# A decode kernel for gated attention and feed-forward: the sum of the exponentials moved from the end of a group to the next group's join with V

## The chip, the cores and the metric

The kernel runs on one core of a Trainium2 chip. The metric is the device time of one execution in microseconds (us); smaller is better. Engines: TensorE (PE) multiplies matrices, VectorE (DVE) and ScalarE (ACT) work element by element, GpSimd (POOL) only sets constants and merges two semaphores here, and SyncE (SP) issues every transfer from HBM. The engines run side by side and meet only at semaphores.

## The reference

One token passes through an attention block with cached keys and values (32 query heads, 8 key/value groups, 32,768 positions of width 128) and through a gated feed-forward block; a scalar gate mixes both.

```python
g = sigmoid((x * gate_w).sum(-1))
q = x @ wq                                # 32 heads of 128
scores = einsum(q, k) * 128 ** -0.5       # per group: 4 heads, 32768 keys
p = softmax(scores)
a = einsum(p, v) @ wo
b = (silu(x @ w_gate) * (x @ w_up)) @ w_down
return g * a + (1 - g) * b
```

K and V are 8 groups of 8.39 MB each, all in bf16, and are read once.

## The kernel before

SBUF holds five pages of 4.19 MB. Two of them hold a group's K in turn (pages A and B for odd groups, B and C for even ones) and two hold V. One loop over the eight groups runs on each engine (`Fori` in steps of `STEP` = 16, so that one semaphore can count all groups).

In each group TensorE first does `emit_k`. A *fill* is eight fp32 transposes of K from a page into one of two PSUM tiles `pst` (L334); VectorE copies each to SBUF (`ktT`, L695); TensorE then multiplies it with the queries into the scores `ps_sc` (L346), two fills behind (`LAG`). There are 16 fills in a group, eight (`UPP`) from each page; page B is read first. After K comes `emit_v` for the group *before*: 64 matmuls of the exponentials `ET` with V into `ps_o` (L401), which this text calls the join. ACT copies the join to `acc` (L576), and `emit_reduce` (L424) folds it to `ps_m`. `emit_max` (L381, L385) turns the row maxima into one maximum per head on all partitions; VectorE makes the bias `nbias` from it (L721), and ACT computes the 32,768 exponentials of the four heads in eight instructions (L583), each with its sum in `esum`.

Last in the group is `emit_sum`. VectorE adds the two halves of `esum` to `esum2` (L733), TensorE sums it over the partitions (L413, into the bank of the scores), VectorE takes the reciprocal (L737) and multiplies it with the gate (L739). Since TensorE runs in program order, the fills of the next K stand behind this sum, and so behind all exponentials of the group.

SyncE issues transfers in the order K(0), K(1), V(0), K(2), V(1), K(3), V(2) and so on, with a wait before each:

```python
if g > 1:
    sp.wait_ge(sem_fill, UPG * (g - 1) + UPP + (g == 2))   # load_k, L277
...
if g:
    sp.wait_ge(sem_v_free, STEP * (g + 1))                 # load_v
```

K(g) goes when page B of the group before has been read, that is 8 fills into group g-1; for K(2) one fill later, 25 in all instead of 24. V(g) goes when the join of V(g-1) is done. The last V goes in two halves, page by page, then the down weights `wd`, and behind the seventh join the output weights `wo` in five pieces (L326).

After the loop `emit_end` joins the last V, folds it, multiplies by `wd`; VectorE scales by the reciprocals (L749), transposes, and TensorE runs through the pieces of `wo` as they land (L223, L234). One copy (L770) and one transfer end the kernel.

Of the kernel before, what the change touches and what calls it, by code (L numbers as in the profile page):

```python
# [5 lines left out]
ACT = mybir.ActivationFunctionType  # L6
# [6 lines left out]
def bass_gated_mix__gqa_block_cached__swiglu_ffn__decode_kernel(  # L13
# [37 lines left out]
    LAG = 2  # L51
# [26 lines left out]
    with ExitStack() as es:  # L78
        def S_(name):
            return es.enter_context(nc.semaphore(name))  # L80
# [39 lines left out]
        sem_nbias = S_("s_nbias")  # L120
        sem_exp = S_("s_exp")
        sem_v_free = S_("s_v_free")
        sem_es = S_("s_es")
        sem_s = S_("s_s")
        sem_acc = S_("s_acc")
        sem_red = S_("s_red")
        sem_rc = S_("s_rc")
        sem_dve_oT1 = S_("s_dve_oT1")
        sem_dve_oT2 = S_("s_dve_oT2")
# [36 lines left out]
        nbias = T("nbias", [128, HPG], FP32)  # L166
        esum = T("esum", [128, NB, HPG], FP32)
        eone = T("eone", [128, 1], FP32)
        esum2 = T("esum2", [128, HPG], FP32)
        acc = T("acc", [128, RQ, DH], FP32)  # L170
        rS = T("rS", [128, HPG], FP32)
        rSw = T("rSw", [128, (G + 1) * STEP], FP32)
        oTw = T("oTw", [128, (G + 2) * STEP], FP32)
        oTs = T("oTs", [128, H], BF16)
        O2a = T("O2a", [128, WOJ], BF16)
        O2 = T("O2", [128, WOJ], BF16)
# [10 lines left out]
        M_A0 = 0  # L187
        M_B0 = M_A0 + 128
        M_P0 = M_B0 + HPG
        M_T0 = M_P0 + HPG  # L190
        M_O0 = M_T0 + FC
        M_X0 = M_O0 + WOJ
        M_G0 = M_X0 + KC
# [1 line left out]

        ps_i = ps_sc[0][:, 0:128]
        ps_c = ps_sc[0][:, :]
        ps_s = ps_sc[1][:, 0:HPG]
        ps_d = ps_sc[1][:, 0:128]

        strip_sel = ident[:, :].rearrange("p (s x) -> p s x", s=NSTRIP)[:, :, 0]
# [55 lines left out]
        with nc.Block("main") as block:  # L257
# [13 lines left out]
            def _(sp):  # L271
                def load_k(g):
                    lo = PG_A if g % 2 else PG_B
                    dst = page[:, lo : lo + NB, :].rearrange("p b (r d) -> p b r d", d=DH)
                    src = A_k_cache[0, g, :, :].rearrange("(p b r) d -> p b r d", b=NB, r=R)
                    if g > 1:
                        sp.wait_ge(sem_fill, UPG * (g - 1) + UPP + (g == 2))  # L277
                        sp.dma_start(
                            dst.rearrange("p b r d -> p (b r d)"),
                            src.rearrange("p b r d -> p (b r d)"),  # L280
                        ).then_inc(sem_k[0], 16)
                        return
                    for b in range(NB):
                        first = lo + b == PG_B
                        if g and first:
                            sp.wait_ge(sem_fill, UPP)
                        sp.dma_start(dst[:, b, :, :], src[:, b, :, :]).then_inc(
                            sem_k[0] if first else sem_k1 if g else sem_k[1], 16
                        )
# [39 lines left out]
            def _(pe):  # L329
# [25 lines left out]
                def emit_k(i):  # L355
                    pe.wait_ge(sem_k[0], i + 16)
                    for n in range(UPP):
                        if n >= LAG:
                            pe.wait_ge(sem_cp, i + (n - LAG + 1))
                        emit_fill(PG_B, n)  # L360
                        if n >= LAG:
                            emit_scores(0, n - LAG)
                    pe.wait_ge(sem_k[1], i + 16)
                    odd = i & STEP
                    for n in range(UPP, UPG + LAG, LAG):
                        if n < UPG:
                            for pg in (PG_A, PG_C):
                                with pe.If(odd > 0) if pg == PG_A else pe.Else():
                                    for m in range(n, n + LAG):
                                        pe.wait_ge(sem_cp, i + (m - LAG + 1))  # L370
                                        emit_fill(pg, m - UPP)
                        else:
                            pe.wait_ge(sem_cp, i + UPG)
                        for m in range(n - LAG, n):
                            ins = emit_scores(m // UPP, m % UPP)
                            if m % UPP == UPP - 1:
                                ins.then_inc(sem_sc, UPP)
# [30 lines left out]
                            )  # L408
                    ins.then_inc(sem_v_free, STEP)

                def emit_sum(i):
                    pe.wait_ge(sem_es, i + STEP)
                    pe.matmul(  # L413
                        ps_s,
                        ones_f[:, :],
                        esum2[:, :],
                        start=True,
                        stop=True,
                    ).then_inc(sem_s, STEP)

                def emit_reduce(n):
                    pe.wait_ge(sem_acc, n)
                    for q in range(RQ):
                        ins = pe.matmul(  # L424
                            ps_m[:, M_P0 : M_P0 + HPG],
                            acc[:, q, :],
                            sel4[:, q * HPG : (q + 1) * HPG],
                            start=(q == 0),
                            stop=(q == RQ - 1),
                        )  # L430
                    ins.then_inc(sem_red, STEP)

                def emit_start():
# [84 lines left out]
                    pe.wait_ge(sem_ps0, 1)  # L518
                    pe.wait_ge(sem_dve_tT, 1)
                    for n, sem in enumerate((sem_v_free, sem_red)):  # L520
                        c = M_P0 + 2 * n
                        pe.matmul(
                            ps_m[:, c : c + 2],
                            ones_f[0:1, :],
                            ones_f[0:1, 0:2],
                            start=True,
                            stop=True,
                        ).then_inc(sem, STEP)

                    with pe.Fori(0, G * STEP, STEP) as i:  # L530
                        emit_k(i)
                        with pe.If(i > 0):
                            emit_v(
                                [[(sem_v, i), (sem_exp, i)], []], (PG_V, PG_V + 1)
                            )
                            emit_reduce(i + STEP)
                        emit_max(i)
                        emit_sum(i)

                def emit_end():  # L540
                    emit_v(
                        [[(sem_exp, G * STEP), (sem_vl[0], 16)], [(sem_vl[1], 16)]], PG_L
                    )
                    emit_reduce((G + 1) * STEP)
                    pe.wait_ge(sem_ld_wd, 16)
                    for j in range(FC):
# [16 lines left out]
            def _(act):  # L563
# [5 lines left out]
                act.activation(sg, pst[1][:, 0:FS], ACT.Sigmoid).then_inc(sem_act_sg, 1)  # L569

                act.wait_ge(sem_ones, 2)
                act.activation(eone[:, :], ones_f[:, 0:1], ACT.Exp)

                with act.Fori(0, G * STEP, STEP) as i:
                    act.wait_ge(sem_v_free, i + STEP)
# [19 lines left out]
            def _(dve):  # L595
# [92 lines left out]
                dve.wait_ge(sem_pe_t, 1)  # L688
                dve.tensor_copy(tT[:, :], ps_m[:, M_T0 : M_T0 + FC]).then_inc(sem_dve_tT, 1)

                with dve.Fori(0, G * STEP, STEP) as i:
                    for n in range(UPG + 1):
                        if n < UPG:
# [18 lines left out]
                    dve.wait_ge(sem_t, i + STEP)  # L712
                    dve.tensor_reduce(  # L713
                        gm[:, :], ps_m[0:HPG, M_A0 : M_A0 + 128], AX.X, ALU.max
                    ).then_inc(sem_d, 1)
                    dve.wait_ge(sem_d, i + 3)
                    dve.tensor_scalar(  # L717
                        diag[:, :], ident_f[0:HPG, 0:HPG], gm[:, 0:1], None, op0=ALU.mult
                    ).then_inc(sem_dg, STEP)
# [1 line left out]
                    dve.tensor_scalar(  # L721
                        nbias[:, :], ps_m[:, M_B0 : M_B0 + HPG], -SCALE, None, op0=ALU.mult
                    ).then_inc(sem_nbias, STEP)
                    dve.wait_ge(sem_red, i + STEP)
                    dve.tensor_scalar(
                        oTw[:, bass.ds(i, HPG)],
                        ps_m[:, M_P0 : M_P0 + HPG],
                        1.0,
                        None,
                        op0=ALU.mult,  # L730
                    ).then_inc(sem_rc, STEP)
                    dve.wait_ge(sem_exp, i + STEP)
                    dve.tensor_tensor(  # L733
                        esum2[:, :], esum[:, 0, :], esum[:, 1, :], ALU.add
                    ).then_inc(sem_es, STEP)
                    dve.wait_ge(sem_s, i + STEP)
                    dve.reciprocal(rS[:, :], ps_s).then_inc(sem_d, 1)  # L737
                    dve.wait_ge(sem_d, i + 4)
                    dve.tensor_scalar(  # L739
                        rSw[:, bass.ds(i, HPG)], rS[:, :], g_col[:, 0:1], None, op0=ALU.mult  # L740
                    ).then_inc(sem_d, STEP - 4)

                dve.wait_ge(sem_red, (G + 1) * STEP)
                dve.tensor_copy(
                    oTw[:, G * STEP : G * STEP + HPG], ps_m[:, M_P0 : M_P0 + HPG]
                ).then_inc(sem_rc, STEP)
                dve.wait_ge(sem_rc, (G + 1) * STEP)
                dve.wait_ge(sem_d, G * STEP)
                dve.tensor_tensor(  # L749
                    oTs[:, :].rearrange("p (g h) -> p g h", h=HPG),  # L750
                    oTw[:, STEP : (G + 1) * STEP].rearrange("p (g x) -> p g x", x=STEP)[:, :, 0:HPG],
                    rSw[:, 0 : G * STEP].rearrange("p (g x) -> p g x", x=STEP)[:, :, 0:HPG],
                    ALU.mult,
                ).then_inc(sem_dve_oT1, 1)
                dve.wait_ge(sem_dve_oT1, 1)
                dve.transpose(O2a[:, :], oTs[:, :]).then_inc(sem_dve_oT2, 1)
# [48 lines left out]
```

## Time and profile before

| | |
|---|---|
| median of three runs | 353.12 us (352.42 to 355.97) |
| profiled execution: time / span | 353.74 us / 352.4 us |
| busy, share of the span: PE, PEld, DVE, ACT | 75%, 63%, 54%, 9% |
| mean granted TensorE clock | 0.831 |
| moved by the DMA queue | 148.12 MB, 97.9% of 16 engines' span |

The span runs from the first to the last instruction on the core. PE is a matmul, PEld the load of its stationary operand, which overlaps it. A row of a group or of the timeline gives line, engine, operation, result and operands, count and time; in square brackets or behind the last bar stands the idle time just before and what ended it. A plain fp32 matmul shows as two passes ("x2").

### The profile page before, as it was taken

Reading aid. Unit: us, or ns where it says so; the run is one execution under the profiler, and the core shown is the slowest. Engines: PE = TensorE matmul, PEld = TensorE weight load, DVE = VectorE, ACT = ScalarE, POOL = GpSimd, SP = SyncE. Lnnn points to the kernel's source line nnn. Section 1 sums busy time; section 2 is a strip of 40 time slices with the busy share of each in tenths; the row PEclk is TensorE's granted clock in tenths of the full one; section 3 lists DMA queues with packets and bytes.
Section 4 is the critical chain, followed back from the end, with each engine's and each line's share of the span. In section 5 each row is a group of like instructions: output and inputs, shape, how many; then the busy total and the mean of one; then the engine's idle time right before and its main releaser. Section 6 shows DMA issues by size and latency. Waiting matters only on the chain.

```text
span 352.4 us, 8780 instructions
## 1 busy us (share of the span) xinstructions
PE 263.5 (75%) x3875; PEld 221.1 (63%) x3875; DVE 190.0 (54%) x251; ACT 33.4 (9%) x143; POOL 0.4 (0%) x6
## 2 busy tenths in 40 slices
PE   1445994399939995899759983999379963999383
PEld 1125994399529972898359942996279843995231
DVE  4134894199417960598129921795149921894100
ACT  1002000300040002100030003000400012000400
POOL 0000000000000000000000000000000000000000
PEclk9975898589887996699759985898859995898878
DMA  8999999998899999998998998999999989989996
GB/s 340 400 448 420 456 424 438 433 402 335 379 476 439 394 476 402 431 476 372 461 469 365 476 461 372 476 439 394 476 402 431 476 365 469 469 365 435 419 422 241
DMA packets 4051, 148.22 MB, mean 421 GB/s; under 512 B 458, under 2 KB 460, under 8 KB 844
## 3 DMA queue, kind: packets, MB, share of 16 engines
q1 hardware_dynamic: 4044, 148.12, 97.9%
q8 instruction: 6, 0.10, 0.1%
q14 instruction: 1, 0.01, 0.0%
HBM read 148.11 MB, written 0.00 MB: 420 GB/s over the span
## 4 chain that ended last, share of the span: by engine, by line
DMA 45%; PE 44%; issue 4%; DVE 3%; ACT 2%; SPq 1%; ACTq 0%; DVEq 0%
DMA page<-in_A_k_cache_dram 39%; PE pst L334 30%; PE ps_sc L346 8%; DMA page<-in_A_wo_dram 6%; PE ps_o L401 4%; ACT ET L583 2%; DVE ktT L695 2%; PE ps_m L424 1%; PE ps_sc L413 0%; SPq L326 0%; PE ps_m L385 0%; ACT acc L576 0%; DVE gm L713 0%; SPq L311 0%; ACTq L583 0%
## 5 line engine op out<-in xcount | busy, mean ns | idle before, releaser
L695 DVE COPY ktT<-pst 128x2048 bf16<-128x2048 bf16 x128 | 153.5, 1221 | 34.8 <-PE pst L334 30.5
L334 PE MATMUL pst<-ident_f,page 128*128 128x128 f32 x1024 | 148.8, 301 | 7.6 <-DMA page<-in_A_k_cache_dram 6.4
L334 PEld LDWEIGHTS pst<-ident_f,page 128*128 128x128 f32 x1024 | 127.7, 156 | 11.5 <-DMA page<-in_A_k_cache_dram 6.9
L346 PE MATMUL ps_sc<-qcur,ktT 128*128 128x8 bf16 x2048 | 64.2, 166 | 6.3 <-DVE ktT L695 6.3
L346 PEld LDWEIGHTS ps_sc<-qcur,ktT 128*128 128x128 bf16 x2048 | 63.8, 97 | 8.0 <-DVE ktT L695 7.0
L401 PE MATMUL ps_o<-page,ET 128*16 128x512 bf16 x512 | 41.2, 494 | 0.4 <-issue 0.4
L401 PEld LDWEIGHTS ps_o<-page,ET 128*16 128x16 bf16 x512 | 15.1, 110 | 22.7 <-issue 16.5
L583 ACT ACTIVATE ET<-ps_sc,nbias 128x128 bf16 x64 | 23.9, 556 | 52.3 <-DVE nbias L721 52.3
L413 PE MATMUL ps_sc<-esum,ones_f 128*128 128x4 f32 x16 | 4.5, 351 | 31.1 <-DVE esum L733 31.1
L576 ACT ACTIVATE acc<-ps_o 128x512 f32<-128x512 f32 x8 | 4.8, 597 | 223.9 <-PE ps_o L401 219.9
L713 DVE TENSOR_REDUCE gm<-ps_m 4x1 f32<-4x128 f32 x8 | 2.2, 278 | 43.9 <-PE ps_m L381 43.9
L413 PEld LDWEIGHTS ps_sc<-esum,ones_f 128*128 128x128 f32 x16 | 4.0, 312 | 31.5 <-issue 31.5
L583 ACT ACTIVATION_READ_ACCUMULATOR ET<-ps_sc,nbias 128x1 f32 x64 | 18.3, 286 | 0.0
L703 DVE TENSOR_REDUCE pmaxf<-ps_sc 128x4 f32<-128x512 f32 x16 | 11.0, 686 | 8.4 <-PE ps_sc L346 8.4
L733 DVE TENSOR_TENSOR esum<-esum 128x4 f32<-128x4 f32 x8 | 1.3, 162 | 25.4 <-ACT ET L583 25.4
L424 PEld LDWEIGHTS ps_m<-sel,acc 128*128 128x128 f32 x64 | 7.7, 191 | 10.1 <-ACT acc L576 8.9
L424 PE MATMUL ps_m<-sel,acc 128*128 128x4 f32 x64 | 8.4, 255 | 6.1 <-ACT acc L576 5.3
L385 PE MATMUL ps_m<-diag,ones_f 4*128 4x4 f32 x16 | 3.6, 294 | 6.3 <-DVE diag L717 6.3
L385 PEld LDWEIGHTS ps_m<-diag,ones_f 4*128 4x128 f32 x16 | 3.2, 244 | 7.8 <-issue 7.8
L445 PE MATMUL ps_m<-ones_bf,x_row 1*128 1x1 bf16 x4 | 0.3, 172 | 9.3 <-DMA x_row<-in_A_x_dram 9.3
L445 PEld LDWEIGHTS ps_m<-ones_bf,x_row 1*128 1x128 bf16 x4 | 0.2, 115 | 9.6 <-DMA x_row<-in_A_x_dram 9.6
L381 PE MATMUL ps_m<-ident_f,pmax 128*4 128x128 f32 x8 | 2.3, 282 | 3.7 <-issue 3.7
(73 smaller groups left out, 53.6 us busy)
## 6 DMA issues: line engine op xcount, KB each, us to landing
page<-in_A_k_cache_dram SPq DMA_DIRECT2D x4, 4096.0 KB, 34.5
page<-in_A_v_cache_dram SPq DMA_DIRECT2D x2, 4096.0 KB, 27.9
page<-in_A_wq_dram SPq DMA_DIRECT2D x1, 4096.0 KB, 13.4
page<-in_A_wo_dram SPq DMA_DIRECT2D x1, 2048.0 KB, 18.3
page<-in_B_w_gate_dram SPq DMA_DIRECT2D x1, 1792.0 KB, 16.6
page<-in_B_w_up_dram SPq DMA_DIRECT2D x1, 1792.0 KB, 20.5
wd<-in_B_w_down_dram SPq DMA_DIRECT2D x1, 1792.0 KB, 20.8
page<-in_A_wo_dram SPq DMA_DIRECT2D x1, 1024.0 KB, 20.4
```

The source lines that it names most:

```text
L334: ins = pe.transpose(pst[u % NST][:, k * 128 : (k + 1) * 128], kv[:, n * 128 : (n + 1) * 128], ident_f[:, :],)
L346: ins = pe.matmul(ps_sc[b][:, col : col + 2 * HPG], kt[:, k, e, :], qcur[:, e, :], start=(e == 0), stop=(e == 1),)
L381: pe.transpose(ps_m[0:HPG, M_A0 : M_A0 + 128], pmax[:, :], ident_f[:, :]).then_inc(sem_t, STEP)
L385: pe.matmul(ps_m[:, M_B0 : M_B0 + HPG], ones_f[0:HPG, :], diag[:, :], start=True, stop=True,).then_inc(sem_b, STEP)
L401: ins = pe.matmul(ps_o[32 * c : 32 * c + RQ * HPG, :], ET[:, n : n + RQ, :].rearrange("p n h -> p (n h)"), v[:, k * RQ : (k + 1) * RQ, :], ...
L413: pe.matmul(ps_s, ones_f[:, :], esum2[:, :], start=True, stop=True,).then_inc(sem_s, STEP)
L424: ins = pe.matmul(ps_m[:, M_P0 : M_P0 + HPG], acc[:, q, :], sel4[:, q * HPG : (q + 1) * HPG], start=(q == 0), stop=(q == RQ - 1),)
L576: act.activation(part, ps_o[:, :], ACT.Copy).then_inc(sem_acc, STEP)
L583: act.activation(ET[:, b * R : (b + 1) * R, h], sc[:, h, bass.ds(bank, R)], ACT.Exp, bias=nbias[:, h : h + 1], scale=SCALE, accum_out=esum ...
L695: dve.tensor_copy(ktT[:, n % NKT, :], pst[n % NST][:, :].bitcast(BF16)).then_inc(sem_cp, 1)
L703: dve.tensor_reduce(pmaxf[:, b, :], sc, AX.X, ALU.max).then_inc(sem_d, 1)
L713: dve.tensor_reduce(gm[:, :], ps_m[0:HPG, M_A0 : M_A0 + 128], AX.X, ALU.max).then_inc(sem_d, 1)
```

## The change

- `emit_sum`, `esum2`, `ps_s` and their semaphores go. TensorE goes from the maximum of a group at once to the next group's fills.
- The sum over the partitions is now two accumulating matmuls in `emit_reduce`, one for each half of `esum`, into a column range of its own in `ps_m`. They run one group later, beside the join of the same group's V, ahead of the wait for `acc`.
- Since the next group's scores overwrite what the exponentials read, TensorE waits for `sem_exp` ahead of the first scores of a group, behind its third fill. ACT's first exponential (`eone`) gives the initial count.
- VectorE makes the result of a group in two operations, `emit_out`: the reciprocal from `ps_m`, then one `scalar_tensor_tensor` (fold times gate times reciprocal). It stands after `nbias`, and once after the loop. The scaling of all groups at the end becomes a copy.
- K(2) is issued after 24 fills.

```diff
-                        sp.wait_ge(sem_fill, UPG * (g - 1) + UPP + (g == 2))
+                        sp.wait_ge(sem_fill, UPG * (g - 1) + UPP)
...
                         emit_fill(PG_B, n)
+                        if n == LAG:
+                            pe.wait_ge(sem_exp, i + STEP)
                         if n >= LAG:
                             emit_scores(0, n - LAG)
...
-                def emit_sum(i):
-                    pe.wait_ge(sem_es, i + STEP)
-                    pe.matmul(ps_s, ones_f[:, :], esum2[:, :], ...).then_inc(sem_s, STEP)
                 def emit_reduce(n):
+                    for b in range(NB):
+                        pe.matmul(
+                            ps_m[:, M_S0 : M_S0 + HPG],
+                            ones_f[:, :],
+                            esum[:, b, :],
+                            start=(b == 0),
+                            stop=(b == NB - 1),
+                        )
                     pe.wait_ge(sem_acc, n)
...
                             emit_reduce(i + STEP)
                         emit_max(i)
-                        emit_sum(i)
...
-                        [[(sem_exp, G * STEP), (sem_vl[0], 16)], [(sem_vl[1], 16)]], PG_L
+                        [[(sem_exp, (G + 1) * STEP), (sem_vl[0], 16)], [(sem_vl[1], 16)]], PG_L
+                    pe.wait_ge(sem_rc, G * STEP)
                     emit_reduce((G + 1) * STEP)
...
-                act.activation(eone[:, :], ones_f[:, 0:1], ACT.Exp)
+                act.activation(eone[:, :], ones_f[:, 0:1], ACT.Exp).then_inc(sem_exp, STEP)
...
+                def emit_out(i, at):
+                    dve.wait_ge(sem_red, i + STEP)
+                    dve.reciprocal(rS[:, :], ps_m[:, M_S0 : M_S0 + HPG]).then_inc(sem_rs, STEP)
+                    dve.wait_ge(sem_rs, i + STEP)
+                    dve.scalar_tensor_tensor(
+                        oTw[:, at], ps_m[:, M_P0 : M_P0 + HPG], g_col[:, 0:1], rS[:, :],
+                        ALU.mult, ALU.mult,
+                    ).then_inc(sem_rc, STEP)
...
-                    (wait sem_red, scale oTw; wait sem_exp, esum2 = esum[0] + esum[1];
-                     wait sem_s, rS = 1 / ps_s; rSw = rS * g_col)
+                    emit_out(i, bass.ds(i, HPG))
+                emit_out(G * STEP, slice(G * STEP, G * STEP + HPG))
...
-                dve.tensor_tensor(oTs, oTw, rSw, ALU.mult)
+                dve.tensor_copy(oTs, oTw)
```

(The lines in round brackets and the last two are shortened.)

More of the change, by code (lines that the diff above doesn't have):

```diff
@@ L122, in bass_gated_mix__gqa_block_cached__swiglu_ffn__decode_kernel @@
         sem_v_free = S_("s_v_free")
-        sem_es = S_("s_es")
-        sem_s = S_("s_s")
         sem_acc = S_("s_acc")
         sem_red = S_("s_red")
+        sem_rs = S_("s_rs")
         sem_rc = S_("s_rc")
@@ L168, in bass_gated_mix__gqa_block_cached__swiglu_ffn__decode_kernel @@
         eone = T("eone", [128, 1], FP32)
-        esum2 = T("esum2", [128, HPG], FP32)
         acc = T("acc", [128, RQ, DH], FP32)
         rS = T("rS", [128, HPG], FP32)
-        rSw = T("rSw", [128, (G + 1) * STEP], FP32)
-        oTw = T("oTw", [128, (G + 2) * STEP], FP32)
+        oTw = T("oTw", [128, (G + 2) * STEP], BF16)
         oTs = T("oTs", [128, H], BF16)
@@ L189, in bass_gated_mix__gqa_block_cached__swiglu_ffn__decode_kernel @@
         M_P0 = M_B0 + HPG
-        M_T0 = M_P0 + HPG
+        M_S0 = M_P0 + HPG
+        M_T0 = M_S0 + HPG
         M_O0 = M_T0 + FC
@@ L197, in bass_gated_mix__gqa_block_cached__swiglu_ffn__decode_kernel @@
         ps_c = ps_sc[0][:, :]
-        ps_s = ps_sc[1][:, 0:HPG]
         ps_d = ps_sc[1][:, 0:128]
@@ L409, in emit_v @@
                     ins.then_inc(sem_v_free, STEP)
-                def emit_sum(i):
-                    pe.wait_ge(sem_es, i + STEP)
[L413 to L419, printed above, removed]
-                def emit_reduce(n):
+                def emit_reduce(n):
+                    for b in range(NB):
[6 more added lines that the diff above has]
+                        )
                     pe.wait_ge(sem_acc, n)
@@ L520, in emit_start @@
                     for n, sem in enumerate((sem_v_free, sem_red)):
-                        c = M_P0 + 2 * n
+                        c = M_P0 + HPG * n
                         pe.matmul(
-                            ps_m[:, c : c + 2],
+                            ps_m[:, c : c + HPG],
                             ones_f[0:1, :],
-                            ones_f[0:1, 0:2],
+                            ones_f[0:1, 0:HPG],
                             start=True,
@@ L533, in emit_start @@
                             emit_v(
-                                [[(sem_v, i), (sem_exp, i)], []], (PG_V, PG_V + 1)
+                                [[(sem_v, i)], []], (PG_V, PG_V + 1)
                             )
@@ L689, in _ @@
                 dve.tensor_copy(tT[:, :], ps_m[:, M_T0 : M_T0 + FC]).then_inc(sem_dve_tT, 1)
+                def emit_out(i, at):
[3 more added lines that the diff above has]
+                    dve.scalar_tensor_tensor(
+                        oTw[:, at],
+                        ps_m[:, M_P0 : M_P0 + HPG],
+                        g_col[:, 0:1],
+                        rS[:, :],
+                        ALU.mult,
+                        ALU.mult,
+                    ).then_inc(sem_rc, STEP)
                 with dve.Fori(0, G * STEP, STEP) as i:
@@ L714, in _ @@
                         gm[:, :], ps_m[0:HPG, M_A0 : M_A0 + 128], AX.X, ALU.max
-                    ).then_inc(sem_d, 1)
-                    dve.wait_ge(sem_d, i + 3)
+                    ).then_inc(sem_d, STEP - 2)
+                    dve.wait_ge(sem_d, i + STEP)
                     dve.tensor_scalar(
@@ L723, in _ @@
                     ).then_inc(sem_nbias, STEP)
[L724 to L749, printed above, removed]
+                    emit_out(i, bass.ds(i, HPG))
+                emit_out(G * STEP, slice(G * STEP, G * STEP + HPG))
+                dve.wait_ge(sem_rc, (G + 1) * STEP)
+                dve.tensor_copy(
                     oTs[:, :].rearrange("p (g h) -> p g h", h=HPG),
-                    oTw[:, STEP : (G + 1) * STEP].rearrange("p (g x) -> p g x", x=STEP)[:, :, 0:HPG],
-                    rSw[:, 0 : G * STEP].rearrange("p (g x) -> p g x", x=STEP)[:, :, 0:HPG],
-                    ALU.mult,
+                    oTw[:, STEP : (G + 1) * STEP].rearrange("p (g x) -> p g x", x=STEP)[
+                        :, :, 0:HPG
+                    ],
                 ).then_inc(sem_dve_oT1, 1)
```

## The prediction

> **What bounds the kernel now.** I read the page's totals first, then its DMA parts, because no engine is busy for more than 75% of the span.
>
> ```profile
> span 352.4 us, 8780 instructions
> PE 263.5 (75%) x3875; PEld 221.1 (63%) x3875; DVE 190.0 (54%) x251; ACT 33.4 (9%) x143; POOL 0.4 (0%) x6
> ...
> q1 hardware_dynamic: 4044, 148.12, 97.9%
> ```
>
> One queue moves 148.12 MB and its packets fill 97.9% of the span of all 16 DMA engines. That points to a transfer-bound kernel, so the next view is the table of windows: does the stream ever stop? Columns: the window in us, its length, busy time of each engine, TensorE clock, DMA share, GB/s (a packet counts where it starts).
>
> ```profile
> 40.00:78.00 38.00, 27.91 (x441) 26.64 (x440) 24.69 (x30) 3.00 (x16) 0.00 (x0) 0.82 1.02 435
> 78.00:79.00 1.00, 1.00 (x23) 0.99 (x22) 0.91 (x2) 0.00 (x0) 0.00 (x0) 1.00 0.91 393
> 79.00:80.00 1.00, 1.00 (x22) 0.99 (x21) 0.91 (x2) 0.00 (x0) 0.00 (x0) 1.00 0.00 0
> 80.00:81.00 1.00, 1.00 (x17) 0.90 (x13) 1.00 (x1) 0.00 (x0) 0.00 (x0) 1.00 0.00 0
> 81.00:82.00 1.00, 0.99 (x10) 0.86 (x9) 0.91 (x2) 0.00 (x0) 0.00 (x0) 1.00 0.00 0
> 82.00:140.00 58.00, 47.87 (x747) 39.70 (x745) 32.94 (x43) 5.26 (x25) 0.00 (x0) 0.86 1.01 434
> 140.00:200.00 60.00, 51.12 (x741) 46.32 (x742) 38.60 (x44) 5.51 (x29) 0.00 (x0) 0.82 1.01 437
> 200.00:260.00 60.00, 44.21 (x660) 35.94 (x657) 28.07 (x41) 7.18 (x34) 0.00 (x0) 0.80 1.01 436
> ```
>
> The stream runs at 434 to 437 GB/s and stops exactly once, from 79 to 82 us. The issues of the SyncE queue and the time from issue to landing say why. First the timeline of the queue, then, in the same order, the landing rows of those five issues (last number: us to landing).
>
> ```profile
> 44.67 0.33 SPq L287 DMA_DIRECT2D page<-in_A_k_cache_dram  x1
> 45.04 0.43 SPq L298 DMA_DIRECT2D page<-in_A_v_cache_dram  x1
> 81.17 0.33 SPq L278 DMA_DIRECT2D page<-in_A_k_cache_dram  x1
> 97.94 0.33 SPq L298 DMA_DIRECT2D page<-in_A_v_cache_dram  x1
> 117.11 0.33 SPq L278 DMA_DIRECT2D page<-in_A_k_cache_dram  x1
> ```
>
> ```profile
> page<-in_A_k_cache_dram SPq DMA_DIRECT2D x1, 4096.0 KB, 17.3
> page<-in_A_v_cache_dram SPq DMA_DIRECT2D x1, 36.3
> page<-in_A_k_cache_dram SPq DMA_DIRECT2D x1, 22.1
> page<-in_A_v_cache_dram SPq DMA_DIRECT2D x1, 24.6
> page<-in_A_k_cache_dram SPq DMA_DIRECT2D x1, 24.8
> ```
>
> Issue plus landing time gives the landings: second half of K(1) 61.97, V(0) 81.34, K(2) 103.27, V(1) 122.54, K(3) 141.91. The steps between them are 19.37, **21.93**, 19.27 and 19.37 us. V and K of a group are 8.39 MB each, so 19.34 us is the streaming time of one and K(2) cost 2.59 us more: it was issued at 81.17, when V(0) was already at its end. Its lone landing time of 22.1 is 19.34 plus 2.76 of start and completion that nothing covered. So a transfer loses nothing if it is issued 2.76 us before its predecessor lands; for K(2) that is by 78.58.
>
> **The change, part by part.** The waits of the engines show what the removed sum cost TensorE, and what it already waits for beside it.
>
> ```profile
> PE ps_sc L413 <- DVE esum L733: 31.1, 8, 3.9
> PE pst L334 <- DMA page<-in_A_k_cache_dram: 6.4, 4, 2.8
> ```
>
> 31.1 us of TensorE idle time in eight groups look like a large prize. But the second row says that in four of the groups TensorE, once past the sum, waits for K all the same, and the stream between 82 and 260 us never pauses. A TensorE that is ready earlier then only waits longer for K. The one place where its lateness stops the stream is K(2), which waits for fills of group 1. The timeline of TensorE and the exponentials (ACT) there:
>
> ```profile
> 63.46 0.56 PE L385 MATMUL ps_m<-diag,ones_f 4*128 4x4 f32 x2 [0.79 <-DVE diag L717]
> 64.49 0.55 ACT L583 ACTIVATE ET<-ps_sc,nbias 128x128 bf16 x1 [31.76 <-DVE nbias L721]
> 67.17 0.31 ACT L583 ACTIVATION_READ_ACCUMULATOR ET<-ps_sc,nbias 128x1 f32 x1
> 67.90 0.56 PE L413 MATMUL ps_sc<-esum,ones_f 128*128 128x4 f32 x2 [3.88 <-DVE esum L733]
> 68.39 4.88 PE L334 MATMUL pst<-ident_f,page 128*128 128x128 f32 x24
> 78.75 1.07 PE L334 MATMUL pst<-ident_f,page 128*128 128x128 f32 x8
> 80.07 2.17 PE L334 MATMUL pst<-ident_f,page 128*128 128x128 f32 x16
> ```
>
> *Next K at once.* Fills of group 1 start 0.49 us after the start of the sum's two passes (67.90 to 68.39). With the sum gone, the same two-pass broadcast of the maximum at 63.46 is last, and K(1) has been there since 61.97: fills start at 63.95, **4.44 us sooner**. The new wait, for all exponentials before the first scores, stands behind three fills: these end at 63.95 + 4.88 = 68.83, the exponentials at 67.48, so it costs nothing with 1.35 us to spare. Were that cover gone it would delay the fourth fill, and with it K(2), by the excess. The copies of the first fills now run while ACT reads its scores, which the trace of before does not show; bound: nothing, up to a doubling of the 2.99 us of exponentials, which would hold the scores 1.64 us. I take nothing, and the slack below covers the other end.
>
> *K(2) after 24 fills.* A fill is eight passes: 16 fills belong to group 0, three to the 24 passes from 68.39, then one every 1.31 us, so the row at 78.75 is fill 24, ending at 79.82, and the first half of the row at 80.07 is fill 25, behind which K(2) went at 81.17. One fill fewer is 1.35 us sooner. With both edits K(2) is issued at 81.17 - 1.35 - 4.44 = **75.38**, 3.2 us ahead of 78.58. "At once" alone gives 76.73, also early enough; 24 fills alone give 79.82 and leave 1.24 us of the gap. So the second edit adds nothing beyond the first; together they remove the whole 2.59.
>
> *The sum moved beside V's join.* Two fp32 products per group (two passes each) go in ahead of the wait for ACT's copy of the join. The rows that price them and their cover, with the end of the kernel, where alone they lie near the last chain:
>
> ```profile
> 334.40 5.81 PE L401 MATMUL ps_o<-page,ET 128*16 128x512 bf16 x64 [0.39 <-issue]
> 340.97 1.05 PE L424 MATMUL ps_m<-sel,acc 128*128 128x4 f32 x8 [0.76 <-ACT acc L592]
> 342.13 0.16 DVE L744 COPY oTw<-ps_m 128x4 f32<-128x4 f32 x1 [7.54 <-PE ps_m L424]
> 343.14 0.19 DVE L758 CAST O<-ps_m 128x32 bf16<-128x32 f32 x1 [0.38 <-PE ps_m L550]
> 344.96 1.03 PE L223 MATMUL ps_sc<-page,O 128*1 128x512 bf16 x16 [1.86 <-DMA page<-in_A_wo_dram]
> 349.97 0.38 PE L234 MATMUL ps_sc<-page,O 128*1 128x128 bf16 x8 [0.24 <-DMA page<-in_A_wo_dram]
> ```
>
> A pair of passes took 0.56 at the low clock (67.90), so two sums are 1.12 at most, against 0.76 of idle time: 0 to 0.36 us remain. On VectorE, a group loses one esum addition and two scalings and gains one fused operation:
>
> ```profile
> L673 DVE SCALAR_TENSOR_TENSOR ktT<-ktT,og_col,pst 128x448 bf16<-128x448 f32 x1 | 0.7, 681 | 0.0
> L739 DVE TENSOR_SCALAR rSw<-rS,g_col 128x4 f32 x8 | 1.8, 229 | 1.0
> L737 DVE RECIPROCAL rS<-ps_sc 128x4 f32<-128x4 f32 x8 | 1.5, 183 | 6.0 <-PE ps_sc L413 6.0
> ```
>
> The fused operation on four columns is not shown: at most the 0.68 of its form on 448 columns, at least the 0.16 of a copy on four; I take the 0.23 of the scaling, the nearest row by size. Behind the join of the last group the chain then holds a reciprocal of 0.18, 0.13 of semaphore (1.0 over 8 in the scaling's row) and 0.23 where it held a copy of 0.16: 0.38 more (0.83 with the larger price), plus the 0.36. It ends at 343.33 now, and TensorE then waits until 344.96 for output weights: 1.63 us of cover, more than the 0.7 to 1.2 added, and the join itself no longer stands behind the sum at 333. Price zero. Without the cover it would be those 0.7. In the loop the two operations take 0.54 us ahead of the first copy, whose fill takes 1.63 (4.88 over 3) anyway.
>
> *What is late next.* After K(2), V(1) waits for the join of V(0): 97.94 - 4.44 = 93.5, where 103.27 - 2.59 - 2.76 = 97.9 is needed. K(3) goes some 4.6 us sooner with K(2)'s fills (112.5), needed by 122.54 - 2.59 - 2.76 = 117.2. So the margins are over 4 us and no stop moves there. From group 2 on TensorE waits for K.
>
> *A rule weighed.* The lone K(2) shows 2.76 us of start and completion. The Trainium skill ("DMA: Bandwidth & Descriptors", Anatomy of one DMA) puts the fixed cost of a DMA, measured there on the GpSimd path, at about 2.0 us beside its bytes over 436 GB/s, most of it the confirmation of the last write. By that figure, an estimate, the stop would have cost 81.17 + 2.0 - 81.34 = 1.83 us and the forecast would be 351.3. The trace has its own duration for the same thing, so its 2.76 goes into the sum.
>
> **Sum.** 2.59 us less in the span of 352.4: 349.8. The profiled execution took 353.74, so 351.15 for it. It lay 0.62 above the median of the three runs, 353.12; from that I forecast **350.5 us**, 0.7% less. For the other end of the gain: from 40 to 82 us the windows hold 38 x 435 + 393 = 16,923 kB where 42 x 434 = 18,228 would fit, so the engines on average lost 3.0 us: 350.1. The runs of before spread 0.7 below their median.
>
> **Rivals.**
> *Only part of the gap closes* (351.0 to 351.8). If TensorE stalls at the loop's end for code, as the 3.66 us "issue" pause ahead of the first maximum of group 0 lets one fear, fills start at 67.6, K(2) goes at 79.0 and 0.5 is lost: 351.0. If the start does not move at all, only the 24 fills count: 1.24 lost, 351.8. Against it: the present jump back costs no more than 0.49 us.
>
> ```profile
> 62.30 0.37 PE L381 MATMUL ps_m<-ident_f,pmax 128*4 128x128 f32 x1 [3.66 <-issue]
> ```
>
> *TensorE's waits come back in full*: seven groups by 3.9 us, 27 us, about 326. For it speak the 31.1 us of the first wait row. Against it: 148.12 MB at 434 GB/s need 341 us by themselves.
>
> *Slower: the transfers lose pace* because fills, copies and exponentials now overlap one another and the arriving pages. K(2) to K(7) and V(1) to V(7) follow, thirteen times 8.39 MB; 0.20 us each (1%) eats the gain, and from there on the kernel is slower: 0.5 each gives 353.1 + 6.5 - 2.6 = 357.0. Against it: the step to V(0), in which TensorE stood idle twice (3.66 and 3.88), took 19.37 and that to K(3) 19.37 too, though TensorE was busy for 47.87 of the 58 us around it. Nor do fills overlap exponentials in later groups, where K comes last.
>
> *The change does nothing here* (353.1): if the stop at 79 us were not K(2)'s late issue. The landing row of 22.1 speaks against that.
>
> **How the numbers follow.** Gap closed 0.68, part closed 0.13, nothing 0.06, TensorE's waits back 0.04, slower 0.09. One per cent, 3.5 us, is about what a measurement of this kernel tells from no change. The forecast of 2.6 to 3.0 less lies below that by 0.5 to 0.9, so scatter carries some 0.13 of its 0.68 past it: faster 0.17. Slower 0.07 (some of the lost pace stays under 1%); the same 0.76. The range goes from 350.1 less the 0.7 of scatter, 349.4, to 352.8, which takes in the part-closed case with scatter.
>
> **What would show it.** Right: K(2) issued near 75.4; no window without packets near 80; K(2) landing 19.3 us after V(0); TensorE's wait for the esum gone and its wait for K grown to several us in each group from 2 on; every step between landings 19.3. Wrong: a new stop in the stream, a step over 19.5, exponentials longer than 3 us, or a tail in which the last weights wait for TensorE.

## The result and the profile after

| | before | after |
|---|---|---|
| median, each of 12 runs | 353.48 us | 351.18 us (forecast 350.5) |
| lowest to highest | 352.24 to 356.03 | 351.01 to 352.6 |
| profiled execution: span | 352.4 us | 349.8 us |

The ratio is 0.993, with a 95% interval of 0.9904 to 0.9956: the kernel is 0.7% faster, 2.3 us between the medians and 2.6 us between the two spans. Less expected is the second row of times: the runs of after lie within 1.6 us, those of before within 3.8. In the sets of the experiments, one run of before (577.52 us), one of the kernel with the stall put back (768.38) and three of before (356.47 to 356.99) count as slow, and the ratios leave them out.

The page's totals of after: TensorE is as busy as it was, and the same bytes fill 98.4% of a shorter span.

```profile
span 349.8 us, 8783 instructions
PE 262.9 (75%) x3891; PEld 220.9 (63%) x3891; DVE 187.0 (53%) x236; ACT 33.4 (10%) x143; POOL 0.4 (0%) x6
...
q1 hardware_dynamic: 4044, 148.12, 98.4%
```

The table of windows of after, around the place of the old stop (last columns: TensorE clock, DMA share, GB/s):

```profile
40.00:78.00 38.00, 31.80 (x522) 30.38 (x519) 28.64 (x31) 2.99 (x16) 0.00 (x0) 0.91 1.02 435
78.00:79.00 1.00, 1.00 (x11) 1.00 (x10) 1.00 (x3) 0.00 (x0) 0.00 (x0) 1.00 1.21 524
79.00:80.00 1.00, 1.00 (x35) 0.99 (x34) 1.00 (x2) 0.00 (x0) 0.00 (x0) 1.00 1.06 459
80.00:81.00 1.00, 1.00 (x16) 0.88 (x12) 0.98 (x1) 0.00 (x0) 0.00 (x0) 1.00 1.07 459
81.00:82.00 1.00, 1.00 (x12) 0.95 (x11) 0.84 (x1) 0.00 (x0) 0.00 (x0) 1.00 1.36 590
82.00:140.00 58.00, 43.07 (x659) 34.98 (x657) 27.46 (x37) 7.17 (x34) 0.00 (x0) 0.84 1.00 433
```

The three windows that were empty before now carry 459 to 590 GB/s; rates far over 435 in so short a window only say where packets begin. Next the queue's issues of V(0), K(2) and V(1) in after, and then their landing rows in the same order (last number: us from issue to landing):

```profile
44.20 0.43 SPq L295 DMA_DIRECT2D page<-in_A_v_cache_dram  x1
74.44 0.33 SPq L275 DMA_DIRECT2D page<-in_A_k_cache_dram  x1
92.54 0.33 SPq L295 DMA_DIRECT2D page<-in_A_v_cache_dram  x1
```

```profile
page<-in_A_v_cache_dram SPq DMA_DIRECT2D x1, 37.1
page<-in_A_k_cache_dram SPq DMA_DIRECT2D x1, 26.2
page<-in_A_v_cache_dram SPq DMA_DIRECT2D x1, 27.4
```

V(0) lands at 81.30 (81.34 before), K(2) at 100.64 and V(1) at 119.94: steps of 19.34 and 19.30 where before had 21.93 at K(2). K(2) now goes 6.86 us ahead of V(0)'s landing; before it was 0.17. The text below calls this its *lead*.

TensorE's wait in the waits of after:

```profile
PE pst L331 <- DMA page<-in_A_k_cache_dram: 36.9, 6, 7.0
```

The 31.1 us of waiting for the sum are gone, and the wait for K has grown from 6.4 to 36.9. So 30.5 of the 31.1 us of TensorE time that came free are spent waiting for data.

### The profile page after: what moved, and what is told of

It is laid out like the page before. It is cut to its first block, busy times and chain, and to the rows that moved or that the text cites. A ratio compares the mean times of both kernels' runs of the same rounds, so it can differ in the third digit from the quotient of the medians.

```text
span 349.8 us, 8783 instructions
## 1 busy us (share of the span) xinstructions
PE 262.9 (75%) x3891; PEld 220.9 (63%) x3891; DVE 187.0 (53%) x236; ACT 33.4 (10%) x143; POOL 0.4 (0%) x6
## 3 DMA queue, kind: packets, MB, share of 16 engines
q1 hardware_dynamic: 4044, 148.12, 98.4%
## 4 chain that ended last, share of the span: by engine, by line
DMA 61%; PE 35%; issue 2%; DVE 1%; SPq 1%; DVEq 0%
DMA page<-in_A_k_cache_dram 54%; PE pst L331 26%; PE ps_sc L343 6%; DMA page<-in_A_wo_dram 6%; PE ps_o L400 2%; DVE ktT L705 1%; SPq L323 0%; SPq L308 0%; DVE pmaxf L713 0%; PE ps_m L384 0%; PE ps_sc L231 0%; SPq L304 0%; PE ps_m L380 0%; SPq L305 0%; DVE res_row L759 0%
## 5 line engine op out<-in xcount | busy, mean ns | idle before, releaser
L331 PE MATMUL pst<-ident_f,page 128*128 128x128 f32 x1024 | 148.5, 300 | 37.9 <-DMA page<-in_A_k_cache_dram 36.9
L400 PE MATMUL ps_o<-page,ET 128*16 128x512 bf16 x512 | 40.2, 485 | 3.5 <-ACT ET L580 3.5
L690 DVE RECIPROCAL rS<-ps_m 128x4 f32<-128x4 f32 x9 | 1.6, 182 | 11.1 <-PE ps_m L421 11.1
L412 PEld LDWEIGHTS ps_m<-esum,ones_f 128*128 128x128 f32 x32 | 4.2, 190 | 3.5 <-issue 3.5
L412 PE MATMUL ps_m<-esum,ones_f 128*128 128x4 f32 x32 | 4.9, 258 | 0.0
```

The lines of the kernel that those rows point to most:

```text
L331: ins = pe.transpose(pst[u % NST][:, k * 128 : (k + 1) * 128], kv[:, n * 128 : (n + 1) * 128], ident_f[:, :],)
L400: ins = pe.matmul(ps_o[32 * c : 32 * c + RQ * HPG, :], ET[:, n : n + RQ, :].rearrange("p n h -> p (n h)"), v[:, k * RQ : (k + 1) * RQ, :], ...
L412: pe.matmul(ps_m[:, M_S0 : M_S0 + HPG], ones_f[:, :], esum[:, b, :], start=(b == 0), stop=(b == NB - 1),)
```

## Experiments

Two theories stood against each other. **Theory:** only the moment of K(2)'s issue counts. **Rival:** TensorE's shorter groups give the gain, some 0.3 us in each of eight. All ratios are to the kernel before, with 95% intervals; each set has its own runs of before (medians 353.4 to 353.8).

### The gain without touching TensorE

The kernel before, its sum and every TensorE wait kept; K(2) comes in two halves, so that the stream has 4 MB in hand while page B is being read.

```diff
+                    if g == 2:
+                        sp.wait_ge(sem_fill, UPG)
+                        sp.dma_start(dst[:, 1, :, :], src[:, 1, :, :]).then_inc(sem_k2, 16)
+                        sp.wait_ge(sem_fill, UPG + UPP + 1)
+                        sp.dma_start(dst[:, 0, :, :], src[:, 0, :, :]).then_inc(sem_k[0], 16)
+                        return
```

> The kernel before with its sum and TensorE's wait of 3.9 us in every group kept; K(2) is loaded in two halves, page C's as soon as group 0 has been filled (16 fills), page B's after 25 fills as before. The stream then never runs dry. Theory: the whole 2.6 us are gained without any change on TensorE, ratio 0.993, TensorE's wait for the esum still 31 us. Rival (TensorE's shorter groups): 1.000.

Measured: 351.49 us median, 0.9952 (0.992 to 0.9984). TensorE's wait for the sum in this kernel is untouched:

```profile
PE ps_sc L422 <- DVE esum L742: 31.0, 8, 3.9
```

Issues of K(2)'s two halves and V(1), and their landing rows:

```profile
54.98 0.33 SPq L281 DMA_DIRECT2D page<-in_A_k_cache_dram  x1
79.91 0.33 SPq L283 DMA_DIRECT2D page<-in_A_k_cache_dram  x1
96.68 0.33 SPq L307 DMA_DIRECT2D page<-in_A_v_cache_dram  x1
```

```profile
page<-in_A_k_cache_dram SPq DMA_DIRECT2D x1, 4096.0 KB, 36.1
page<-in_A_k_cache_dram SPq DMA_DIRECT2D x1, 4096.0 KB, 20.9
page<-in_A_v_cache_dram SPq DMA_DIRECT2D x1, 24.3
```

V(0) lands at 81.35, the halves at 91.08 and 100.81, as in after. So the gain is there, 2.3 us between the medians of this set, with all 31 us of TensorE's wait still in place; the rival is out. V(1), with a lead of 4.13 us, lands 20.17 us later: 0.83 lost at a lead that the prediction called safe. Two of the twelve runs, at 354.0 and 354.87, show nothing of the gain; they have no trace.

### TensorE's stall put back

The kernel after, with TensorE waiting for all exponentials ahead of the next fills.

```diff
                         emit_max(i)
+                        pe.wait_ge(sem_exp, i + 2 * STEP)
```

> The kernel after, with TensorE made to wait for all exponentials of a group ahead of the first fill of the next, so that some 3.5 us of the old wait are back in every group; the sum stays where the change put it. Theory: fills of group 1 start near 66.7, K(2) goes near 78.1, half a us ahead of the latest moment, so nothing is lost, ratio 0.993 (0.994 if it slips past). Rival (TensorE's shorter groups): the gain is gone, 1.000.

Measured: 352.42 us median, 0.9968 (0.9933 to 1.0004), between the two expectations; the runs that count reach from 351.13, the time of after, to 355.34. The profiled execution, a fence for each view: the timeline with the first fill of group 1 and the issues of K(2), V(1) and K(3); their landing rows; TensorE's wait.

```profile
66.88 1.54 PE L331 MATMUL pst<-ident_f,page 128*128 128x128 f32 x6 [3.96 <-ACT ET L581]
78.21 0.33 SPq L275 DMA_DIRECT2D page<-in_A_k_cache_dram  x1
96.23 0.33 SPq L295 DMA_DIRECT2D page<-in_A_v_cache_dram  x1
114.95 0.33 SPq L275 DMA_DIRECT2D page<-in_A_k_cache_dram  x1
```

```profile
page<-in_A_k_cache_dram SPq DMA_DIRECT2D x1, 22.6
page<-in_A_v_cache_dram SPq DMA_DIRECT2D x1, 24.1
page<-in_A_k_cache_dram SPq DMA_DIRECT2D x1, 25.0
```

```profile
PE pst L331 <- ACT ET L581: 7.9, 2, 4.0
```

The fills start 3.8 us later than in after (63.08), K(2) goes as forecast (78.1), with a lead of 3.01, and its step is 19.59: 0.25 lost. V(1) and K(3) follow with leads of 4.58 and 5.38 and lose 0.18 and 0.28 more; together that is about the 0.6 by which the span (350.4) exceeds that of after. The stall binds in two groups only, not in every group as expected; in the others K comes last. The times alone decide nothing here, since their interval takes in both 0.994 and 1.000. That the median lies above the theory is put down to the thin lead; what this can do in a single run shows in the 30-fill kernel below.

### The second edit taken apart

```diff
 # kernel before
-                        sp.wait_ge(sem_fill, UPG * (g - 1) + UPP + (g == 2))
+                        sp.wait_ge(sem_fill, UPG * (g - 1) + UPP)
```

> The kernel before, with K(2) issued after 24 fills instead of 25 and nothing else. Theory (only the moment at which K(2) is issued counts: every us by which issue plus 2.76 lies behind V(0)'s landing at 81.3 is lost): K(2) at 79.8, 1.24 us still lost, 1.35 us gained, ratio to before 0.996. Rival (the gain comes from TensorE's shorter groups, 0.3 us in each of eight): ratio 1.000.

Measured: 352.8 us median against 353.81, 0.9994 (0.9964 to 1.0024). In the profiled execution, K(2)'s issue and its landing row:

```profile
80.13 0.33 SPq L278 DMA_DIRECT2D page<-in_A_k_cache_dram  x1
```

```profile
page<-in_A_k_cache_dram SPq DMA_DIRECT2D x1, 21.8
```

This bears the size out: the step is 20.66, 1.32 lost against 2.59. But V(1), with a lead of 3.71, loses 0.25 more, which the expectation left out. The times cannot tell the edit from nothing, and their interval just leaves out the 0.996.

```diff
 # kernel after
-                        sp.wait_ge(sem_fill, UPG * (g - 1) + UPP)
+                        sp.wait_ge(sem_fill, UPG * (g - 1) + UPP + (g == 2))
```

> The kernel after, with K(2) held back to 25 fills again. Theory: K(2) at 75.8, still 2.7 us ahead of the latest moment without loss (78.5), so the time of the kernel after, ratio to before 0.993. If the 24 fills carry part of the gain: 0.996 or so.

Measured: 351.38 us median, 0.9948 (0.9922 to 0.9975); K(2) at 76.24, step 19.38. Within the intervals this is the time of after, but the interval takes in the 0.996 too. That the 24 fills bring nothing beside the earlier start rests on the step, 0.04 over 19.34.

### K(2) held back by force

The kernel after, TensorE's shorter groups kept, K(2) later.

```diff
-                        sp.wait_ge(sem_fill, UPG * (g - 1) + UPP)
+                        sp.wait_ge(sem_fill, UPG * (g - 1) + UPP + 4 * (g == 2))   # or 6 *
```

> The kernel after, with K(2) held back to 28 fills. By the formula of the prediction (loss = issue + 2.76 - V(0)'s landing): K(2) near 79.5, 0.9 us lost, about 352.1. If the edge is soft (some of the 16 engines run dry earlier than the landing, which is the last one's), up to 0.3 more. Rival (TensorE's shorter groups make the gain): 351.2 as after.

Measured: 352.56 us median, 0.9965 (0.9934 to 0.9996). K(2)'s issue and its landing row:

```profile
79.27 0.33 SPq L275 DMA_DIRECT2D page<-in_A_k_cache_dram  x1
```

```profile
page<-in_A_k_cache_dram SPq DMA_DIRECT2D x1, 21.7
```

The step is 19.66: 0.32 lost, where the formula gives 0.72 for this issue and landing. The profiled execution (351.69) was faster than the median, and the interval leaves room for both expectations, so this run decides nothing between them.

> The kernel after, with K(2) held back to 30 fills, later than in the kernel before, while TensorE keeps its shorter groups. Theory: K(2) near 82.1, 3.5 us lost, 354.7, slower than before by 0.3%: ratio 1.003. Rival (TensorE's shorter groups): 351.2, ratio 0.993.

Measured: 355.09 us median, 1.0056 (1.0023 to 1.0088): slower than before, although TensorE waits for no sum. The rival is out a second time. The profiled execution was the slowest of this kernel (358.53, span 357.2), and it shows where lateness comes from: the timeline with the pauses of TensorE in group 0 and the issue of K(2), its landing row, and the windows.

```profile
56.11 1.58 PE L331 MATMUL pst<-ident_f,page 128*128 128x128 f32 x13 [2.30 <-issue]
64.72 0.37 PE L380 MATMUL ps_m<-ident_f,pmax 128*4 128x128 f32 x1 [4.50 <-issue]
86.18 0.33 SPq L275 DMA_DIRECT2D page<-in_A_k_cache_dram  x1
```

```profile
page<-in_A_k_cache_dram SPq DMA_DIRECT2D x1, 21.9
```

```profile
80.00:82.00 2.00, 2.00 (x45) 1.99 (x44) 2.00 (x2) 0.00 (x0) 0.00 (x0) 1.00 0.00 0
82.00:84.00 2.00, 2.00 (x44) 1.99 (x42) 2.00 (x4) 0.00 (x0) 0.00 (x0) 1.00 0.00 0
84.00:86.00 2.00, 2.00 (x26) 1.84 (x23) 1.82 (x2) 0.00 (x0) 0.00 (x0) 1.00 0.00 0
```

With V(0) landing at 81.35 the formula gives a loss of 86.18 + 2.76 - 81.35 = 7.59; the step of 26.73 is 7.39 over 19.34. K(2) is 4.1 us later than the 82.1 expected from after. Two pauses "issue" make 2.25 of it: they took 2.30 and 4.50 us here, 0.89 and 3.66 in the profiled execution of after. TensorE was also 1.1 us late ahead of the first pause, and its first three fills took 5.38 us instead of 4.71. The two pauses of after:

```profile
53.57 1.58 PE L331 MATMUL pst<-ident_f,page 128*128 128x128 f32 x13 [0.89 <-issue]
61.34 0.37 PE L380 MATMUL ps_m<-ident_f,pmax 128*4 128x128 f32 x1 [3.66 <-issue]
```

The ends of both pauses can be set beside the instruction queue: a 16 KB packet of it starts in the windows 51 to 52 and 58 to 59 us of after, and 53 to 54 and 62 to 63 of this kernel. Its row for 53 to 54:

```profile
q8 instruction: 1, 0.02, 6.7%
```

By the packet records of nine traces (all but the two of the next part), the second pause ends 2.65 to 2.67 us after the start of such a packet, whatever its own length (2.26 to 4.50); the first pause (0.20 to 2.30) ends 2.36 to 2.59 us after one. So TensorE seems to wait, in its first pass through the loop, for code that arrives by DMA beside the data. That is a match in time in the traces, not tested by a change of the code; why the packet starts later in some executions is open.

### TensorE made slower in the later groups

The kernel after, with products that nothing reads between the arrival of K and the first fill, in groups 2 to 7.

```diff
                     pe.wait_ge(sem_k[0], i + 16)
+                    with pe.If(i > STEP):
+                        for _ in range(12):        # or 32
+                            pe.matmul(ps_o[:, 0:128], ones_f[:, :], ident_f[:, :], start=True, stop=True)
```

> The kernel after, with twelve fp32 products (128x128, into the join's bank, read by nothing) in TensorE's order behind the arrival of K and ahead of its first fill, in groups 2 to 7: some 3 to 5 us of extra work in each of six groups. Theory: K(3) to K(7) go later by that, but they now go 7 to 8 us before their predecessor lands, so next to nothing is lost: 351.2 to 352. Rival (TensorE's time in a group counts): 18 to 30 us more, 370 to 380.

Measured: 353.36 us median, 1.0 (0.9972 to 1.0027). The group of the products:

```profile
L356 PE MATMUL ps_o<-ident_f,ones_f 128*128 128x128 f32 x144 | 30.6, 405 | 22.7 <-DMA page<-in_A_k_cache_dram 22.7
```

They took 30.6 us in six groups; the median is 2.2 over that of after. The profiled execution was the slowest of this kernel, with a span of 352.8 against 349.8. Of these 3.0 us, K(3), with a lead of 3.45, lost 1.41: it landed 20.75 us after V(1). The four other K steps, with leads of 3.56 to 4.91, lost 0.05 to 0.28. The second half of the last V, issued 3.2 us ahead of its first half's landing, took 11.0 us instead of 9.7. "Next to nothing" was too little, the rival's 18 to 30 far too much.

> The same with 32 products, 8 to 11 us in each of groups 2 to 7 (less what a warmer clock gives back to the fills). Theory: K's margin of 7 to 8 us is used up, the issue falls to within 2.8 us of the predecessor's landing or behind it, and only the excess counts: 1 to 4 us in each of five groups, 355 to 370. Rival (TensorE's time in a group counts): 48 to 66 us more, over 395.

Measured: 366.32 us median, 1.0355 (1.0294 to 1.0417), inside the range of the theory. The group of the products, then K(3)'s issue and its landing row:

```profile
L356 PE MATMUL ps_o<-ident_f,ones_f 128*128 128x128 f32 x384 | 55.2, 317 | 7.7 <-DMA page<-in_A_k_cache_dram 7.7
```

```profile
120.82 0.33 SPq L275 DMA_DIRECT2D page<-in_A_k_cache_dram  x1
```

```profile
page<-in_A_k_cache_dram SPq DMA_DIRECT2D x1, 21.7
```

55.2 us of extra work cost 15.1 over the median of after. K(3) was issued 0.74 us behind V(1)'s landing (120.08) and its step became 22.44; the other four K steps were 20.96 to 21.25 at leads near 0.7. With the 1.62 to 1.91 that these lost, the five K steps make 10.4 of the 15.4 us between the spans (365.2 and 349.8). The five V steps behind them, at leads of 3.6 to 3.9, lost 0.26 to 0.45 each, 2.1 together, and the second half of the last V, issued as its first half landed, 2.2. So TensorE does set the pace here, and nearly all of it by what transfers go out too late.

### More lead than after has

The kernel after with K(2) in two halves besides (page C's behind 16 fills, page B's behind 24).

> The kernel after, with K(2) in two halves besides (page C's behind 16 fills, page B's behind 24), so that the stream has another 4 MB in hand. Theory: the stream already never stops in the kernel after, so more lead brings nothing: 351.1 to 351.3, ratio to before 0.993, landings 19.3 to 19.4 us apart. Rival (the 16 engines still lose a little at K(2) with 6.9 us of lead): up to 0.5 us less than after.

Measured: 351.27 us median (351.13 to 351.44 in nine runs), 0.9935 (0.9908 to 0.9962). No faster than after, so the gain ends with the gap. It does not beat after by its median. Its runs lie within 0.3 us.

## Why the prediction was right

**The bound.** Right: the stream stood once, at K(2). Two halves of K(2) gave the gain with TensorE unchanged, and 30 fills took it away with TensorE improved.

**Next K at once, 4.44 us sooner.** The same places in after (broadcast of the maximum, first fill, first exponential and last read-out, first scores):

```profile
62.56 0.55 PE L384 MATMUL ps_m<-diag,ones_f 4*128 4x4 f32 x2 [0.86 <-DVE diag L727]
63.08 4.71 PE L331 MATMUL pst<-ident_f,page 128*128 128x128 f32 x24
63.59 0.55 ACT L580 ACTIVATE ET<-ps_sc,nbias 128x128 bf16 x1 [30.95 <-DVE nbias L731]
66.27 0.31 ACT L580 ACTIVATION_READ_ACCUMULATOR ET<-ps_sc,nbias 128x1 f32 x1
67.63 0.55 PE L343 MATMUL ps_sc<-qcur,ktT 128*128 128x8 bf16 x16
```

The first fill follows the broadcast by 0.52 us, as taken over from the sum (0.49), and comes 5.3 us sooner than before; the 0.9 beyond the 4.44 are an earlier maximum in this execution. The exponentials take 2.99 us from first to last read-out as before, although VectorE's copy of the first fill runs beside them (65.08 to 66.31): the price of nothing held. The new wait costs nothing.

**K(2) at 75.4, nothing lost.** It went at 74.44, and nothing was lost. The difference is again the maximum, 0.9 us earlier in this execution; with over 3 us in hand it did not matter.

**The tail costs nothing.** Sum products, fold, last copy (`O`), first product with the output weights in after; and the group of the fused operation:

```profile
337.30 0.61 PE L412 MATMUL ps_m<-esum,ones_f 128*128 128x4 f32 x4
338.14 1.05 PE L421 MATMUL ps_m<-sel,acc 128*128 128x4 f32 x8 [0.23 <-ACT acc L589]
340.54 0.19 DVE L747 CAST O<-ps_m 128x32 bf16<-128x32 f32 x1 [0.28 <-PE ps_m L547]
342.36 1.03 PE L220 MATMUL ps_sc<-page,O 128*1 128x512 bf16 x16 [1.86 <-DMA page<-in_A_wo_dram]
```

```profile
L692 DVE SCALAR_TENSOR_TENSOR oTw<-ps_m,g_col,rS 128x4 f32 x8 | 1.8, 222 | 1.1
```

Four passes took 0.61 us, under the 0.76 of idle time, of which 0.23 remain; the bound of 1.12 was nearly twice too high. The fused operation took 0.222, against the 0.23 taken (`oTw` is also bf16 in after and fp32 in before, which the list of the change leaves out). From the start of the fold to the end of the last copy it is 2.59 us instead of 2.36: 0.23 more, where 0.38 was summed. TensorE waits for the output weights for 1.86 us, exactly as before.

**What was off.** First, the edge of 2.76 us. It was read as sharp, from one landing row. Against it, a choice of steps from the profiled executions (loss is the step over 19.34; landings are printed to 0.1 us, and a loss is good to about that):

| transfer | lead, us | loss measured | loss by the formula |
|---|---|---|---|
| 30 fills, K(2) | -4.83 | 7.39 | 7.59 |
| 32 products, K(3) | -0.74 | 3.10 | 3.50 |
| 24 fills alone, K(2) | 1.14 | 1.32 | 1.62 |
| 28 fills, K(2) | 2.04 | 0.32 | 0.72 |
| stall put back, K(2) | 3.01 | 0.25 | 0 |
| 12 products, K(3) | 3.45 | 1.41 | 0 |
| halves of K(2) in before, V(1) | 4.13 | 0.83 | 0 |
| stall put back, V(1) | 4.58 | 0.18 | 0 |
| 25 fills in after, K(2) | 5.12 | 0.04 | 0 |
| stall put back, K(3) | 5.38 | 0.28 | 0 |
| after, K(2) | 6.86 | 0.00 | 0 |

Behind the edge the formula is 0.1 to 0.4 too dear: transfers that start late land 21.7 to 22.1 us after issue, 2.4 to 2.8 over streaming. The Trainium skill ("DMA: Bandwidth & Descriptors", Anatomy of one DMA) gives about 2.0 for the GpSimd path; the runs here lie above it. That the prediction's estimate with this 2.0, 351.3 us, is nearer to the measured 351.18 is chance, since the step at K(2) did shrink by 2.59.

Ahead of the edge losses remain up to a lead of 5.4, and are uneven. With more lead no step lost over 0.1, but for two in the execution with 28 fills (0.35 and 0.14 at leads of 9.1 and 8.5), which lead does not explain. The trace offers one reason for a soft edge. It keeps 16 reports of completion for each transfer, and the landing is the last of them; the first report of V(0) comes 1.8 to 2.2 us ahead of it in the eleven executions. The parts of a transfer that end first thus have some 2 us less lead than the table says, and 2.76 and 2.0 make 4.8 us for all of them, an estimate. It does not explain all: in the 12-product execution K(3)'s last report alone came 1.4 us behind the other fifteen. That the wrong edge did no harm is due to the size of the lead, 6.86; the stall put back had 3.01, safe by the formula, and its median is 1.2 us over that of after.

Second, the forecast treated the spread of the runs as noise about a fixed 2.6 us. The sum for the profiled execution, 351.15, met the measured 351.13. The 0.62 by which the one of before lay above its median was then taken off as well, and that made 350.5 out of it, 0.7 below the measured 351.18. The times of after do not spread that way: with nothing lost at K(2), no run came below 351.01. The gain against a single run of before depends on that run, from 1 to 5 us in the set of the result; in another set the fastest run of before took 351.02, no more than after. With little lead, a longer pause in group 0 can go into the time. The highest counted runs fit that: 358.5 with 30 fills, 356.0 in before, 355.2 with 1.1 us of lead, 353.8 with 2.0, 355.3 with 3.0, 352.7 with 5.1, 352.6 with 6.9 and 351.4 where half of K(2) is in hand as well. But single runs have no trace, so this is argued and not shown, and the halves of K(2) in before, whose V(1) has 4.1, reach 354.9. The rival of a partly closed gap took a real pause as its model but put it at the loop's end, where after shows 0.52 us from the broadcast to the first fill.

## What to carry to other kernels

Where one queue fills 98% of the span, look for the windows in which it does not, and ask which wait ended just then: a wait of 31 us on an engine was worth nothing, one issue that came 3 us too late was worth all. Judge each transfer by its lead over its predecessor's landing, and keep 5 to 6 us of it rather than the bare start-up time: the steps here lost something up to 5.4 us, and the first pass through the code paused for a different time in nearly every profiled execution. If the engine's program is hard to reorder, a cut of the late transfer into two with separate waits did the same here (2.3 us between the medians).

## What the runs showed of the hardware

TensorE paused at two places of its first pass through the loop, for 0.20 to 2.30 and 2.26 to 4.50 us in the nine profiled executions without extra products. The pauses ended 2.36 to 2.59 and 2.65 to 2.67 us after the start of a 16 KB instruction packet. In before and after, transfers of 8.39 MB issued 5.3 us or more ahead of the previous landing landed 19.3 to 19.4 us apart, whether or not TensorE, VectorE and ACT were busy; a pace slowed by the new overlap did not show. The 16 reports of completion of one transfer lay up to 2.0 us apart there.
